# Loading the first batch by another queue: q and k of batch 0 in fp32 by SyncE, A's last products on GpSimd, and a new written order

## The chip, the cores and the metric

The kernel runs on one core of a Trainium2 chip. A core has TensorE (PE, matrix products, with a sequencer row PEld for weight loads), VectorE (DVE), ScalarE (ACT), GpSimd (POOL) and SyncE (SP), which work side by side and wait for each other by semaphores; 16 DMA engines move data between the chip's memory and the core's SBUF. PE writes its results to PSUM, eight banks of 2 KB per partition. The metric is the device time of one execution in microseconds; lower is better.

## The reference

Eight batches of eight heads; 576 tokens of 64 elements per head. A Nystrom attention with 32 landmarks comes first. All inputs are fp32.

```python
q_lm = q.reshape(B, H, 32, 18, 64).mean(axis=3)      # landmarks: mean of 18 tokens
k_lm = k.reshape(B, H, 32, 18, 64).mean(axis=3)
A = softmax(q @ k_lm.T / 8);  Bm = softmax(q_lm @ k_lm.T / 8);  C = softmax(q_lm @ k.T / 8)
Z = Bm.T / (norm1(Bm) * norminf(Bm) + 1e-6)
for _ in range(6):
    Z = 2 * Z - Z @ Bm @ Z
attn = A @ Z @ C @ v
x = attn.transpose(0, 2, 1, 3).reshape(4608, 512)
h = x @ w_in                                         # 512 x 2048
out = relu(h) ** 2 @ w_out                           # 2048 x 512
```

## The kernel before

**The work.** Batches go one after the other through the attention. For each, `attention(b)` makes the landmarks (`lm`), transposes q and k on VectorE (`T`), makes B with its softmax (`B`, `Bmx`, `Bsb`, `Bex`, `Bsu`, `Brc`, `Bml`), the six steps of the inverse (`N` on PE, `U` on VectorE), C (`SC`, `Cmx`, `Cex`, `CT`), C times v (`CV`), Z times that (`Zd`, `Zm`, `ZC`), folds it with `w_in` into one matrix per batch (`W`, copied from PSUM by `We` to `WP`), and makes A with its softmax (`SA`, `Amx`, `Asb`, `Aex`, `Asu`, `Arc`, `Aml`), transposed by `Ap` and copied by `Ab` to `AT`. The feed-forward layer is then `F` (`AT` times `WP`, line 1023), `R` (ReLU, lines 1037 and 1039), `Q` (square, into the buffer `G`, lines 1044 and 1046), and `O` (`G` times `w_out`, line 1063), tile by tile of 128 tokens, `Oe` (copy out of PSUM) and `St` (store by SyncE, line 1076). `F` of a batch overlaps with the attention of the next; G is a ring for two batches.

**Loads.** q and k are loaded by `load_qk` (line 397) in quarters of a batch: t is 0 for q and 1 for k, r is 0 for heads 0 to 3 and 1 for heads 4 to 7. Each is an fp32 block of 128 partitions x 1152 (590 kB), which GpSimd's DMA queue casts on its way to bf16 (288 KB written) in `X[b % 3]`. v (line 413), `w_in` (421), `w_out` (428) and rows of later batches (`XS`, 403) go by the same queue. The queue keeps eight transfers in flight; the ninth issue waits for the first to land, and GpSimd with it.

**Batch 0.** Its two halves of heads are taken apart: heads 4 to 7 first (`lm0.1`, line 480, `SC0.1`), then heads 0 to 3 (`lm0.0`, line 473, and `B0`, which needs both). Batches 0 and 1 make A with the tokens on partitions: a product against a block-diagonal copy of the landmarks (`bk`, line 914; batch 1's is on GpSimd) and a softmax along the free axis. A's last step, `Aml` (line 938), multiplies the exponentials in SBUF (fp32) by the reciprocals of their sums and writes bf16; batch 0 does it in four pieces (two of 256 and two of 320 elements per partition), batch 1 in two (512 and 640).

**The order.** Each step is an `op` with the engines that it may use, a cost on each, what it reads and writes, and for PSUM how many banks. A text `ORDER` lists all of them with the engine (`/A`, `/D`, `/P`) and the bank (`@4`) where there is a choice; a planner (`Plan.schedule`) walks through it, gives each step a start time by its costs, and the instructions are emitted in order of those times. Every engine then works through its own list in order and waits where data is late. The plan's times set the order and nothing else. `fillers` puts products of a matrix of ones (line 1137) into the gaps that the plan shows on PE before the first `O`, so that PE's clock, which the throttle lowers when PE has been idle, stays up.

Of the kernel before, what the change touches and what calls it, by code (L numbers as in the profile page):

```python
# [7 lines left out]
P = 128  # L8
# [45 lines left out]
class Plan:  # L54
# [100 lines left out]

    def fillers(self, until, width, emit):

        busy = sorted((o.start, o.start + o.engs["PE"] + 0.04) for o in self.ops if o.eng == "PE")
        found, at = [], 1.5
        for a, b in busy:  # L160
            if a > until:
                break
            n = int((a - 0.05 - at) / (width if at > 6 else 2 * width))
            if n > 0:
                for j in range(8):
                    if all(h[1] >= a or h[2] <= at - 0.02 for h in self.history if h[0] == j):
                        found.append((at, j, n))
                        break
            at = max(at, b)
        for at, j, n in found:  # L170
            o = Op()
            o.name, o.eng, o.start, o.mode = f"fill{at:.0f}", "PE", at, "full"
# [9 lines left out]
T0 = {"PE": 1.1, "ACT": 1.1, "DVE": 1.1, "POOL": 1.31, "SP": 1.1}  # L182
SW0, LAND, LOADED = 1.5, 1.75, 140.0
# [53 lines left out]
def kernel(  # L237
# [155 lines left out]
    def load_qk(b, t, r):  # L393
# [4 lines left out]
           W=[("X", b % 3, t, r)], nbytes=589824, queue="sw")  # L398
# [8 lines left out]
    def load_v(b):  # L407
        vv = V[b % 3]
        for r in range(2):
            for i, (p0, c0, n) in enumerate(runs(lambda c: pos_c(c, r))):  # L410
# [4 lines left out]
                   W=[("V", b % 3, r, i)], nbytes=147456 * n, queue="sw")  # L415


    def load_win(r, ch):
# [4 lines left out]
           W=[("win", r, ch)], nbytes=524288, queue="sw")  # L423
# [8 lines left out]
    def attention(b):  # L432
        x, tt, lm, lt = X[b % 3], TT[b % 2], LM[b % 2], LT[b % 2]
        kx = lambda t, r: ("X", b % 3, t, r)
# [5 lines left out]
        def transposes(t):  # L440
            for r in range(2):
# [3 lines left out]
                   R=[kx(t, r)], W=[kt(t, r)])  # L445
# [19 lines left out]
        def landmarks(rs):  # L465
# [4 lines left out]
            def lmx(e):  # L470
# [14 lines left out]
               R=["ident", *[kx(t, r) for t in range(2) for r in rs]], W=[pl_], alloc=[pl_],  # L485
# [406 lines left out]
        for u in range(2) if b in TOKENS else ():  # L892
# [28 lines left out]
            for j, (x0, x1) in enumerate(zip(cuts, cuts[1:])):  # L921
# [15 lines left out]
                op(f"Aml{b}.{u}{z}", {"DVE": v_(w)}, lambda e, sa3=sa3, b3=b3, anv=anv, at=at:  # L937
                   nc.vector.tensor_tensor(anv.rearrange("p (x m) -> p x m", m=M)[:, at], sa3[:, at],  # L938
                                           b3(2)[:, at], ALU.mult),
                   R=[*kx_("sa"), *kx_("arc")], W=kx_("An"))  # L940
# [176 lines left out]

    for b in range(4):
        loads("win", b)
        loads("wout", b)  # L1120
    for b in range(B):
        if b in ROWS:
            loads("xs", b)
        loads("kq", b)
# [177 lines left out]
```

## Time and profile before

| | us |
|---|---|
| median of the runs (lowest, highest) | 267.36 (266.87, 269.35) |
| profiled execution | 268.07 |
| its span, first to last instruction | 266.3 |
| busy PE / PEld | 254.8 / 140.4 |
| busy DVE / ACT / POOL | 210.7 / 185.9 / 75.1 |
| mean granted clock of PE | 0.993 |

The profile is of one execution; the span begins with its first instruction. Busy PE includes the fillers (14.1 us in 40 products) and counts a product until its modelled end, so that PE can be held up while it counts as busy. The chain that ended last is followed back from the last instruction, at each step to what released it. In rows of the timeline, "[2.32 <-DMA X<-in_q_dram]" says that the engine had been idle for 2.32 us until a load of q landed; an `x18` behind a row joins 18 instructions.

### The profile page before, as it was taken

The numbers are of one execution on the slowest core, as the hardware profiler recorded it, in microseconds if no ns is written. First come the engines' busy times: TensorE is split into PE (matmuls) and PEld (weight loads), VectorE is DVE, ScalarE is ACT, GpSimd is POOL, SyncE is SP. The second block draws the span as 40 slices with busy tenths as digits, with TensorE's granted clock in tenths as the row PEclk, the third lists the DMA queues.
The fourth block names the chain that finished last, engine by engine and source line by source line (L and its number), as shares of the span: only waits on it lengthen the run. The fifth ranks groups of instructions, "written<-read, shape, count | busy, mean of one in ns | idle before, by whom it ended". The sixth has DMA issues, their size and how long they took to land.

```text
span 266.3 us, 7555 instructions
## 1 busy us (share of the span) xinstructions
PE 254.8 (96%) x3090; PEld 140.4 (53%) x3090; DVE 210.7 (79%) x539; ACT 185.9 (70%) x339; POOL 75.1 (28%) x121
## 2 busy tenths in 40 slices
PE   7699899999999999999999999999999999999993
PEld 2265566466454566455444556456454555456552
DVE  3399999856899889897998889888899895787311
ACT  1055599978687799899597759899586847667120
POOL 8445389346400362026423220210032102000000
PEclk9799999999999999999999999999999999999999
DMA  5999999997998699919996993213250330017016
GB/s 89 195 196 208 203 201 190 205 182 116 157 234 160 120 165 210 182 41 186 225 224 104 193 178 98 47 15 79 51 114 2 83 81 0 2 34 164 2 47 151
DMA packets 25123, 34.18 MB, mean 128 GB/s; under 512 B 2432, under 2 KB 14464, under 8 KB 25088
## 3 DMA queue, kind: packets, MB, share of 16 engines
q0 software_dynamic: 19168, 24.25, 55.7%
q1 hardware_dynamic: 5840, 9.38, 13.8%
q8 instruction: 24, 0.39, 0.6%
q10 hardware_dynamic: 80, 0.07, 0.1%
q14 instruction: 11, 0.09, 0.1%
HBM read 48.50 MB, written 9.44 MB: 218 GB/s over the span
## 4 chain that ended last, share of the span: by engine, by line
PE 73%; DVE 13%; ACT 6%; issue 3%; DMA 3%; POOL 0%; DVEq 0%; POOLq 0%; ACTq 0%
PE ps L1063 40%; PE ps L1023 20%; ACT RS L1037 3%; DMA X<-in_k_dram 3%; PE ps L859 2%; PE ps L702 2%; DVE TT L442 2%; PE ps L788 2%; ACT G L1044 2%; PE ps L1137 1%; DVE sm L740 1%; DVE WP L388 1%; DVE ST L680 1%; PE ps L666 1%; DVE An L938 1%
## 5 line engine op out<-in xcount | busy, mean ns | idle before, releaser
L1063 PE MATMUL ps<-w_out,G 128*128 128x512 bf16 (+1 forms) x592 | 138.5, 374 | 0.1
L1063 PEld LDWEIGHTS <-G 128*128 128x128 bf16 x592 | 54.1, 98 | 53.3 <-issue 5.4
L1023 PE MATMUL ps<-AT,WP 128*128 128x288 bf16 (+2 forms) x512 | 75.0, 286 | 0.9 <-DVE AT L996 0.3
L1037 ACT ACTIVATE RS<-ps 128x576 bf16<-128x576 f32 (+2 forms) x97 | 60.9, 652 | 19.3 <-PE ps L1023 12.0
L1023 PEld LDWEIGHTS <-WP 128*128 128x128 bf16 x512 | 47.9, 98 | 23.8 <-issue 4.3
L1044 ACT ACTIVATE G<-RS 128x576 bf16<-128x576 bf16 (+2 forms) x78 | 52.3, 687 | 0.7
L603 POOL TENSOR_TENSOR BD<-ST,blkb 128x256 bf16<-128x256 bf16 x21 | 14.9, 710 | 85.6 <-DVE ST L680 44.1
L384 ACT COPY OS<-ps 128x512 f32<-128x512 f32 (+2 forms) x29 | 16.2, 567 | 16.7 <-PE ps L1063 16.5
L442 DVE STREAM_TRANSPOSE TT<-X 128x576 uint32<-128x576 uint32 x32 | 23.8, 758 | 5.1 <-DMA X<-in_k_dram 2.8
L1039 DVE TENSOR_SCALAR RS<-ps 128x576 bf16<-128x576 f32 (+2 forms) x31 | 23.1, 754 | 5.4 <-PE ps L1023 5.1
L384 ACT CAST WP<-ps 128x1024 bf16<-128x1024 f32 (+1 forms) x25 | 22.8, 949 | 3.3 <-PE ps L859 3.2
L743 ACT ACTIVATE C<-ps,sm 128x576 bf16<-128x576 f32 x16 | 14.2, 905 | 12.8 <-DVE sm L740 10.8
L1046 DVE TENSOR_TENSOR G<-RS 128x576 bf16<-128x576 bf16 (+2 forms) x42 | 18.8, 452 | 3.6 <-ACT RS L1037 3.4
L680 DVE SCALAR_TENSOR_TENSOR ST<-ST,ps 128x128 bf16<-128x128 bf16 (+1 forms) x48 | 12.7, 264 | 8.2 <-PE ps L666 8.0
L1137 PE MATMUL ps<-onesb 128*128 128x512 bf16 (+1 forms) x40 | 14.1, 470 | 1.8 <-DVE onesb L320 1.5
L413 POOL DMA_DIRECT2D V<-in_v_dram x24 | 13.0, 543 | 7.5 <-DMA X<-in_q_dram 3.5
L388 DVE COPY OS<-ps 128x512 f32<-128x512 f32 (+1 forms) x9 | 5.8, 640 | 10.8 <-PE ps L1063 9.4
L740 DVE TENSOR_REDUCE sm<-ps 128x1 f32<-128x576 f32 x16 | 11.7, 747 | 1.6 <-PE ps L702 1.6
L976 DVE STREAM_TRANSPOSE SA<-ps 128x320 f32<-128x320 f32 (+1 forms) x24 | 10.1, 459 | 3.5 <-PE ps L697 2.4
L603 POOL TENSOR_TENSOR BD<-Bt,blkb 128x256 bf16<-128x256 bf16 x4 | 3.0, 744 | 30.9 <-DVE sm L597 15.0
L1046 POOL TENSOR_TENSOR G<-RS 128x512 bf16<-128x512 bf16 (+1 forms) x8 | 8.8, 1101 | 9.3 <-DVE RS L1039 5.9
L388 DVE CAST WP<-ps 128x1024 bf16<-128x1024 f32 x9 | 10.8, 1205 | 0.8 <-PE ps L859 0.8
(139 smaller groups left out, 303.9 us busy)
## 6 DMA issues: line engine op xcount, KB each, us to landing
out_dram<-OS SPq DMA_DIRECT2D x70, 128.0 KB, 2.4
X<-in_q_dram POOLq DMA_DIRECT2D x16, 288.0 KB, 9.2
X<-in_k_dram POOLq DMA_DIRECT2D x16, 288.0 KB, 9.3
XS<-in_q_dram POOLq DMA_DIRECT2D x5, 576.0 KB, 11.0
XS<-in_k_dram POOLq DMA_DIRECT2D x5, 576.0 KB, 10.2
V<-in_v_dram POOLq DMA_DIRECT2D x8, 288.0 KB, 10.0
w_in<-in_moe_w_in_dram POOLq DMA_DIRECT2D x8, 256.0 KB, 10.6
w_out<-in_moe_w_out_dram POOLq DMA_DIRECT2D x4, 512.0 KB, 10.2
```

The costliest lines, as they stand in the source:

```text
L384: nc.scalar.copy(o, i)
L388: eng(e).tensor_copy(o, i)
L442: op(f"T{b}.{t}{r}", {"DVE": v_(576)}, lambda e, r=r: nc.vector.transpose(tt[:, t, r].rearrange("p s m e -> p (s m e)").bitcast(U32), x[:, ...
L603: bdiag = lambda e, o, i: eng(e).tensor_tensor(o.rearrange("p r (c m) -> p r c m", c=4), i.unsqueeze(2).to_broadcast([P, 2, 4, M]), blkb[: ...
L680: nc.vector.scalar_tensor_tensor(out=o, in0=i0, scalar=2.0, in1=bank(pN)[:, 0:2 * w].rearrange("p (r w) -> p r w", r=2), op0=ALU.mult, op1 ...
L1023: nc.tensor.matmul(ps[:, ph.at + i, 0:w], lhsT=wp[:, r, 128 * ff:128 * ff + 128], rhs=at[:, r, t0:t0 + w], start=(r == 0), stop=(r == 1))
L1037: nc.scalar.activation(rs, pair(ph, w), AF.Relu)
L1039: nc.vector.tensor_scalar(out=rs, in0=pair(ph, w), scalar1=0.0, scalar2=None, op0=ALU.max)
L1044: nc.scalar.activation(g, rs, AF.Square)
L1046: eng(e).tensor_tensor(g, rs, rs, ALU.mult)
L1063: nc.tensor.matmul(bank(po)[:, 0:c1 - c0], lhsT=G[:, f, lo:lo + P], rhs=w_out[:, f, c0:c1], start=(f == 0), stop=(f == NF - 1))
L1137: nc.tensor.matmul(ps[:, j, 0:w], lhsT=onesb[:, 0:P], rhs=onesb[:, 0:w], start=True, stop=True)
```

## The change

Three things. First, the four quarters of q and k of batch 0 are no longer loaded by GpSimd's queue: SyncE loads them in fp32 into planes of `G` that are not in use yet (`load_first`), in the order q0.1, k0.1, k0.0, q0.0, and eight casts of 128 x 576, four on ScalarE and four on VectorE, bring them to `X[0]`. GpSimd's first loads (q and k of batch 1, v of batches 0 and 1, `w_in`) now name the landing of q0.1 as something that they read, so GpSimd waits for it before its first issue; their order is new as well. Second, `Aml` of batches 0 and 1 may go to GpSimd, and all six pieces do. Third, the filler routine chooses by a share of use in any 3.41 us how many products each gap gets (36 products instead of 40), and the whole `ORDER` is another one, with other choices of engine and bank throughout; the planner's start values for SyncE and for GpSimd's queue are other ones too.

```diff
@@ loads
+    def first(t, r):
+        return G[:, 4 * t + 2 * r:4 * t + 2 * r + 2].rearrange("p f n -> p (f n)").bitcast(F32)
+
+    def load_first(t, r):
+        src = (q, k)[t][0, 4 * r:4 * r + 4].rearrange("c (m s) d -> (c m) (s d)", s=SEG)
+        op(f"ld{'qk'[t]}0.{r}", {"SP": 1.5}, lambda e: nc.sync.dma_start(first(t, r), src), W=[("XF", t, r)])
+        for j in range(2):
+            at = slice(576 * j, 576 * j + 576)
+            op(f"cs{t}{r}.{j}", {"DVE": v_(576, True), "ACT": a_(576)}, lambda e, at=at: copy(
+                e, X[0][:, t, r].rearrange("p s d -> p (s d)")[:, at], first(t, r)[:, at]),
+               R=[("XF", t, r)], W=[("X", 0, t, r, j)])
...
-           W=[("X", b % 3, t, r)], nbytes=589824, queue="sw")
+           R=[("XF", 0, 1)] if b < 2 else [], W=[("X", b % 3, t, r, j) for j in range(2)], nbytes=589824, queue="sw")
...
-                    load_qk(b, t, r)
+                    load_qk(b, t, r) if b else load_first(t, r)
@@ A's last product
-                op(f"Aml{b}.{u}{z}", {"DVE": v_(w)}, lambda e, sa3=sa3, b3=b3, anv=anv, at=at:
-                   nc.vector.tensor_tensor(anv.rearrange("p (x m) -> p x m", m=M)[:, at], sa3[:, at],
+                op(f"Aml{b}.{u}{z}", {"DVE": v_(w), "POOL": g_(w)}, lambda e, sa3=sa3, b3=b3, anv=anv, at=at:
+                   eng(e).tensor_tensor(anv.rearrange("p (x m) -> p x m", m=M)[:, at], sa3[:, at],
                                            b3(2)[:, at], ALU.mult),
-                   R=[*kx_("sa"), *kx_("arc")], W=kx_("An"))
+                   R=[*kx_("sa"), *kx_("arc")], W=kx_("An"), port=("POOL", "DVE"))
@@ planner
-T0 = {"PE": 1.1, "ACT": 1.1, "DVE": 1.1, "POOL": 1.31, "SP": 1.1}
-SW0, LAND, LOADED = 1.5, 1.75, 140.0
+T0 = {"PE": 1.1, "ACT": 1.1, "DVE": 1.1, "POOL": 1.31, "SP": 2.9}
+SW0, LAND, LOADED = 6.6, 1.75, 140.0
@@ fillers
+        times = [6.5 + 0.25 * i for i in range(int(4 * (until - 10)))]
+        for _ in range(80):
+            t = min(times, key=share)
+            near = [g for g in gaps if t <= g[0] < t + 3.41 and g[3] - g[0] - g[1] * g[4] > -0.05]
+            if share(t) >= 0.42 or not near:
+                break
+            g = max(near, key=lambda g: g[3] - g[0] - g[1] * g[4])
+            g[1] += 1
@@ the order, its first lines
-c0 ldq0.1 c1 c2 ldk0.1 c3 lm0.1@2 lmc0.10 c12 T0.01 c17 Bce0@5 ldq0.0 ldk0.0 ldq1.0 ldk1.0 c5
-ldq1.1 ldk1.1 c9 c13 c15 T0.11 c6 lmc0.11/D lme0.1 lmt0.1 SC0.1@0 T0.00 Cmx0.1 T0.10 win31 win00
+c0 ldq0.1 c1 c2 c12 c11 cs01.0/A c5 c18 c3 c9 ldq1.0 c6 cs01.1 T0.01 c17 Bce0@0 ldv0.11 ldk0.1
+cs11.1 c13 c15 cs11.0/A lm0.1@2 T0.11 lmc0.10/D lmc0.11/D lme0.1 lmt0.1 SC0.1@2 ldq1.1 ldk1.0
+ldk1.1 ldk0.0 cs10.1/A cs10.0 ldq0.0 cs00.1/A cs00.0 lm0.0@1 T0.10 Cmx0.1 T0.00 T1.00 lme0.0
+lmt0.0 B0@4 ldv0.00 ldv0.10 win10 win00 win11 win31 win01 T1.01 Bmx0 bk0 Bsb0 Bex0 SC0.0@6 Cmx0.0
...
+ldv1.10 bk1/P win30 ldv1.11 ldq2.1 Bsb1 Asu0.0a N0.3@0 U0.3 N0.4@4 CR0@6 Arc0.0a Bex1 Bsu1 Asb0.0b
+Aex0.0b Brc1 CRe0/A Aex0.1b U0.4 Bmb1 Bml1 Btr1 Asu0.0b N0.5@7 U0.5 Zd0@7 Blo1 Bcs1@0 Aml0.0a/P
```

More of the change, by code (lines that the diff above doesn't have):

```diff
@@ L154, in schedule @@
         return max(o.end for o in self.order)
+    USE = {"N": 0.06, "M": 0.06, "B": 0.06, "Bce": 0.28, "Bcs": 0.3, "BBT": 0.08, "SC": 0.2, "CR": 0.06, "lm": 0.48,
+           "SA": 0.78, "CV": 0.63, "Zd": 0.6, "ZC": 0.2, "Ap": 0.54, "W": 0.9}
     def fillers(self, until, width, emit):
[L158 to L161, printed above, removed]
-                break
[L163 to L169, printed above, removed]
@@ L171, in fillers @@
+        for at, n, j, _, unit in gaps:
+            if not n:
+                continue
             o = Op()
-            o.name, o.eng, o.start, o.mode = f"fill{at:.0f}", "PE", at, "full"
+            o.name, o.eng, o.start, o.mode = f"fill{at:.2f}", "PE", at, "full"
             o.engs, o.end = {"PE": n * width}, at + n * width
@@ L1116, in loads @@
             load_wout(b)
+    loads("kq", 0)
     for b in range(4):
@@ L1123 @@
             loads("xs", b)
-        loads("kq", b)
+        if b:
+            loads("kq", b)
         loads("v", b)
```

213 lines of the change are left out of this document (112 added, 101 removed).

## The prediction

> **What bounds the kernel now.** First the page: how long, and what the chain of waits that ended last is made of.
>
> ```profile
> span 266.3 us, 7555 instructions
> ...
> PE 73%; DVE 13%; ACT 6%; issue 3%; DMA 3%; POOL 0%; DVEq 0%; POOLq 0%; ACTq 0%
> ```
>
> Three quarters of the chain is TensorE (PE). It does not say which part of the run is open to a change of the loads, so next comes busy time by stretches (columns: stretch, length, busy of PE, PEld, DVE, ACT, POOL, granted clock, DMA share, GB/s).
>
> ```profile
> 5.00:10.00 5.00, 2.81 (x43) 1.17 (x41) 1.97 (x7) 0.00 (x0) 2.70 (x7) 1.00 1.02 171
> 10.00:15.00 5.00, 4.75 (x42) 2.32 (x43) 3.39 (x8) 1.30 (x5) 2.11 (x6) 0.66 1.10 207
> 16.42:31.86 15.44, 13.86 (x280) 8.50 (x272) 15.34 (x61) 8.14 (x26) 7.98 (x13) 1.00 1.18 205
> 35.00:40.00 5.00, 4.97 (x64) 3.09 (x57) 4.92 (x14) 5.00 (x10) 3.76 (x5) 1.00 1.17 203
> ```
>
> Three stages: until 10 us everything waits for data; from 16.4 to 31.9 VectorE (DVE) is full while PE passes its time with filler products; from 35 ScalarE (ACT) and VectorE are both full and real feed-forward products run. The DMA engines are full from 10 us on in all of them. The chain, in order of time, and four places of the timeline give the marks that I move:
>
> ```profile
> 2.36 6.80 DMA X<-in_k_dram
> 9.30 0.70 PE ps L480 x36
> ...
> 13.45 1.27 PE L473 MATMUL ps<-X,ident 128*128 128x128 bf16 x18
> 16.42 0.22 DVE L533 TENSOR_REDUCE sm<-ps 128x2 f32<-128x64 f32 x1
> 27.73 0.37 DVE L814 TENSOR_TENSOR ZM<-ps,CRS 128x256 bf16<-128x256 f32 x1
> 31.86 0.61 PE L1023 MATMUL ps<-AT,WP 128*128 128x256 bf16 x4
> ```
>
> The first chain piece is k of heads 4 to 7 on its way (the second load). At 9.30 the first landmark product (lm0.1) can start, at 13.45 the second (lm0.0, which needs all four loads), at 16.42 VectorE takes the maxima of B (Bmx0) and begins a chain without a pause that reaches the first feed-forward product (F0) at 31.86.
>
> **The change, part by part.**
>
> *1. Four loads by SyncE.* When GpSimd may issue again shows when old transfers landed (it keeps eight in flight, so its twelfth issue waits for the fourth load, and so on):
>
> ```profile
> 1.31 0.72 POOL L397 DMA_DIRECT2D X<-in_q_dram  x1 [0.79 <-POOLq L1286]
> ...
> 12.27 0.54 POOL L413 DMA_DIRECT2D V<-in_v_dram  x1 [0.40 <-DMA X<-in_k_dram]
> ...
> 15.06 0.62 POOL L421 DMA_DIRECT2D w_in<-in_moe_w_in_dram  x1 [0.86 <-DMA X<-in_k_dram]
> 16.48 0.62 POOL L421 DMA_DIRECT2D w_in<-in_moe_w_in_dram  x1 [0.80 <-DMA X<-in_q_dram]
> ```
>
> The first issue is at 1.31. Load four has landed at 12.27, six and seven at 15.06 and 16.48, 1.42 us apart. No fp32 load by SyncE is in this trace. Its price has bounds from these rows (the waits of SyncE's queue, the DMA issues, the queues):
>
> ```profile
> SPq L1286 <- PEq L1286: 0.7, 1, 0.7
> out_dram<-OS SPq DMA_DIRECT2D x70, 128.0 KB, 2.4
> q1 hardware_dynamic: 5840, 9.38, 13.8%
> ```
>
> SyncE is free at 0.7; a store of 131 kB lands 2.4 us after its issue; a load is 590 kB, 459 more. Rate: hardware-queue packets took 13.8% of 266.3 = 36.7 us for 9.38 MB, 255 kB/us; the upper bound is what the software queue reads, twice the 203 GB/s that it writes in bf16, 406 kB/us. I take 330, between the two. q0.1 then lands at 0.7 + 2.4 + 1.4 = 4.5 (4.2 to 4.9), each further one 1.8 us later (1.45 to 2.3): 6.3, 8.1, 9.9 if alone. They are not alone: GpSimd now waits for q0.1 before its first load, with batch 1's q and k, all of v and w_in, and its own later products behind that wait. In the run before its first bytes moved about 1.4 us after the issue of 1.31 (the row of 2 to 3 us below), so from about 6 us two queues share the engines. The 1.25 MB that SyncE's still has to bring at half of 406 take 6.2 us: the last lands at 12.3, where the fourth landed before. Bounds: 8.6 (406, unshared) and 17.5 (255 alone, then half of that).
>
> Each load is cast in two halves of 128x576, one on ACT, one on DVE, side by side:
>
> ```profile
> L390 DVE TENSOR_SCALAR C<-C,sm 128x576 bf16<-128x576 bf16 x7 | 2.8, 393 | 0.1
> L384 ACT CAST AT<-ps 128x512 bf16<-128x512 f32 x2 | 1.2, 603 | 0.8 <-PE ps L949 0.8
> ```
>
> 0.39 us, or 0.68 with the second row scaled to 576, for a half; I take 0.65. All eight lie where DVE and ACT wait for data (1.97 and 0 busy of 5 above), except the last pair, which is on the path. lm0.1 starts at 6.3 + 0.65 = 7.0 instead of 9.30, lm0.0 at 12.3 + 0.65 = 13.0 instead of 13.45. From lm0.0's end to Bmx0 the old order needed 1.7 us (14.72 to 16.42), for VectorE was still busy with heads 4 to 7; these are now past. lm0.0 (1.0), its copy and transpose (0.5) and one transpose of batch 1 that now stands before Bmx0 (T1.01, 0.77) give Bmx0 at 15.3 to 15.4: **1.0 us gained**. T1.01 needs q1.1, now 6 1/4 loads into the stream: 15.06 + 0.36 = 15.4 by the old pace. The stream runs ahead of the old one by as much as it moves more in the first 6 us:
>
> ```profile
> 2.00:3.00 1.00, 1.00 (x4) 0.38 (x3) 0.50 (x2) 0.09 (x1) 0.91 (x4) 1.00 0.38 32
> 3.00:4.00 1.00, 1.00 (x3) 0.30 (x2) 0.00 (x0) 0.00 (x0) 1.00 (x3) 1.00 0.96 168
> 4.00:5.00 1.00, 1.00 (x4) 0.39 (x3) 0.00 (x0) 0.00 (x0) 1.00 (x3) 1.00 0.93 145
> 5.00:6.00 1.00, 1.00 (x4) 0.37 (x3) 0.72 (x1) 0.00 (x0) 0.93 (x4) 1.00 0.79 136
> ```
>
> That was 481 kB written by 6 us, 0.96 MB read; at 330 kB/us from about 2 us on, 1.32 MB are moved by then, 0.36 MB or 0.9 us at 406 more, say 1.0 with the earlier issue. q1.1 at 14.4 is just in time for a DVE that wants it at 14.5. Without that lead DVE stands up to 1 us there.
>
> *2. A's last products on GpSimd.* From Bmx0 to F0 VectorE is busy 15.34 of 15.44 us (the row above), so what leaves it counts:
>
> ```profile
> 25.36 1.40 DVE L561 TENSOR_TENSOR Bb<-Bl,sm 128x64 bf16<-128x64 f32 x1
> 25.50 1.16 POOL L914 TENSOR_TENSOR BK<-LT,blkw 128x512 bf16<-128x512 bf16 x1
> 27.32 0.38 DVE L938 TENSOR_TENSOR An<-SA,smA 128x256 bf16<-128x256 f32 x1
> 28.02 0.41 DVE L938 TENSOR_TENSOR An<-SA,smA 128x256 bf16<-128x256 f32 x1
> 28.48 0.77 DVE L442 STREAM_TRANSPOSE TT<-X 128x576 uint32<-128x576 uint32 x1
> 29.41 0.87 DVE L938 TENSOR_TENSOR An<-SA,smA 128x320 bf16<-128x320 f32 x2
> ...
> 18.12 0.22 DVE L561 TENSOR_TENSOR Bb<-Bl,sm 128x64 bf16<-128x64 f32 x1
> ...
> 16.12 0.38 DVE L914 TENSOR_TENSOR BK<-LT,blkw 128x512 bf16<-128x512 bf16 x1
> 15.76 0.43 DVE L749 STREAM_TRANSPOSE CT<-C 128x288 uint32<-128x288 uint32 x1
> ```
>
> Gone: batch 0's four products 0.38 + 0.41 + 0.87 = 1.66, T1.01 (moved ahead, paid above) 0.77, and the stall: Bb took 0.22 at 18.12 but 1.40 beside GpSimd's BK, 1.18 more. BK is now behind 15 software loads instead of 22, at the time of A's maxima and subtractions, which read PSUM; I count the stall as gone and keep 1.2 us as its price if it falls on such a product again. Added behind Bmx0: BK 0.38, one CT transpose 0.43. Net 2.80. Rows overlap at their hand-overs (by about 0.1 each), so I count **2.2 us**. On GpSimd the nearest row is
>
> ```profile
> L603 POOL TENSOR_TENSOR BD<-ST,blkb 128x256 bf16<-128x256 bf16 x21 | 14.9, 710 | 85.6 <-DVE ST L680 44.1 <-DVE ST L627 41.5
> ```
>
> 0.7 each for 256, 0.9 for 320. They stand in GpSimd's order behind the issue of batch 2's first load, the 18th, which waits for its tenth to land. Seven loads (4.13 MB) had landed at 16.48; the tenth ends at 7.47 MB (four by SyncE, ten behind them), 8.2 us later at 406, less the lead: 23.7 us, when A's sums are about ready. If it is late by x, the first feed-forward product is late by x.
>
> The Trainium skill's page "SBUF — State Buffer" (Who interferes with whom) says that a VectorE instruction with two SBUF inputs and a GpSimd instruction that reads SBUF exclude each other for the whole instruction. The 1.40 agrees. By it each of the six moved products (two are batch 1's) can block VectorE's next such product; at 1.18 each that would be 7 us against the gain here, and this trace shows one such stall in the stretch.
>
> *3. How much arrives.* F0 would begin 1.0 + 2.2 = 3.2 us earlier. But the second feed-forward matrix is not moved up: the same bytes stand before it.
>
> ```profile
> 34.35 1.58 POOL L428 DMA_DIRECT2D w_out<-in_moe_w_out_dram  x2
> 45.94 1.03 PE L1063 MATMUL ps<-w_out,G 128*128 128x512 bf16 x4
> DMA to landing us min/median/max: 9.5/10.2/11.4
> ```
>
> The first row is the issue of two quarters, the last (of w_out's own view) the time from issue to landing. The first quarter lands at 43.9 to 44.6 and is used at 45.94: 1.4 to 2.1 us of cover, plus the stream's lead of 1.0, is 2.4 to 3.1. PE takes its products in order, so beyond that it waits. **2.7 us** of the 3.2 arrive.
>
> *4. The order after 50 us, and fillers.* Counted in the written order, VectorE takes 11 squares and 5 ReLUs over (8 squares and the ReLUs from ACT):
>
> ```profile
> L1039 DVE TENSOR_SCALAR RS<-ps 128x576 bf16<-128x576 f32 (+2 forms) x31 | 23.1, 754 | 5.4 <-PE ps L1023 5.1
> L1046 DVE TENSOR_TENSOR G<-RS 128x576 bf16<-128x576 bf16 (+2 forms) x42 | 18.8, 452 | 3.6 <-ACT RS L1037 3.4
> ```
>
> 11 at 0.45 and 5 at 0.75 are 8.7 us; its other exchanges (the casts and three output copies against three WP and the six A products) about cancel. PE's products are the same. DVE and ACT carry 13% and 6% of the chain, so I count 0, with 2 us either way. The fillers are 36 instead of 40 and stand at other places; they matter through the clock (0.66 in the row of 10 to 15 above), at a time when VectorE sets the pace: 0, at most 1 us.
>
> Sum: 2.7 us off the profiled execution (268.07 with what lies around its span) is 265.4; off the median of 267.36 it is **264.7**.
>
> **Rivals.**
>
> - *SyncE's loads have the engines to themselves longer, and the new order is as good behind them.* lm0.0 at 9.9 + 0.65, gain 2.9 there, 5 at F0; w_out allows 3.1 plus up to 0.5 of lead, and the rest up to 2: 263.8 to 261.8. For it: the DMA share was below 1 until 6 us. Against: two queues.
> - *Sharing eats the front.* The last load is late, since GpSimd's queue takes half: 14.9 is the point from which lm0.0 (15.6) cancels the 2.2 of part 2. At 17.5 it is 4.7 late, 2.5 net. The four loads at 255 also put the stream behind by 3.4, more than w_out's cover; with one stall of 1.2 on the port this gives 269.9 to 272. For it: k's load took 6.80 us in company, in the chain's first row. Against: at the middle rate it stays hidden.
> - *VectorE becomes the bound.* The 8.7 us that it takes over fall partly on stretches where it was full; half on the chain is 4.3 less the 2.7: 269, or 268 to 270.6.
> - *Nothing is won at the loads.* Only part 2 remains, limited by the cover of 1.4 to 2.1 without a lead: 265.6. The Trainium skill's page "DMA: Bandwidth & Descriptors" (Issuing engines are not separate DMA queues) states as much: all queues run on the same 16 engines and only issue time is saved. The shares near 1 above bear it out from 6 us on, not before.
>
> **How the numbers follow.** A change of 1%, 2.7 us, is about what can be told from none. Forecast 0.36 (own range 263.2 to 266.2, more than half below 264.7), loads alone 0.20, sharing 0.21, VectorE 0.13, nothing won 0.10. Faster: 0.22 + 0.20 = 0.42. Slower: 0.21 + 0.06 = 0.27. The rest, 0.31, is within 1%. The range reaches from 261.0 to 271.5.
>
> **What would show it.** Right: lm0.1 at about 7, lm0.0 near 13, Bmx0 near 15.4, the first product of F0 at 28 to 29, the first of w_out at 43 to 43.5, and the same distance to the end. Wrong: lm0.0 after 15, GpSimd's first An after 26, PE waiting on w_out by more than 1 us, or ground lost between 50 and 250 with a chain that has more of VectorE.

## The result, and the profile after

| | before | after |
|---|---|---|
| median of 20 runs each, us | 268.06 | 266.38 |
| lowest, highest | 265.19, 270.69 | 264.97, 267.02 |
| profiled execution, its span | 268.07, 266.3 | 266.46, 264.7 |

The ratio of after to before is 0.9933, 95% interval [0.9911, 0.9955]: 0.7% less time, about 1.8 us, where 2.7 were forecast. The interval excludes no change, and the gain is still within the 1% that the prediction named as hardly to be told from none. The lowest times are alike; what differs is the upper end, 270.69 against 267.02.

The changed kernel's page, its length and the chain that ended last; then its busy time by stretches (columns as before: stretch, length, busy of PE, PEld, DVE, ACT, POOL, granted clock, DMA share, GB/s):

```profile
span 264.7 us, 7514 instructions
...
PE 69%; DVE 16%; ACT 10%; issue 4%; ACTq 0%
```

```profile
5.00:10.00 5.00, 2.89 (x43) 1.71 (x44) 3.48 (x11) 2.19 (x5) 2.38 (x5) 0.76 1.04 314
14.60:30.31 15.71, 14.24 (x277) 8.69 (x271) 14.45 (x59) 8.00 (x22) 8.88 (x14) 0.82 1.18 198
21.00:23.00 2.00, 1.12 (x50) 0.59 (x36) 2.00 (x9) 0.93 (x3) 2.00 (x4) 1.00 1.24 204
24.00:25.00 1.00, 1.00 (x13) 0.38 (x11) 1.00 (x7) 0.82 (x4) 0.00 (x0) 0.82 1.03 167
25.00:30.00 5.00, 4.87 (x69) 2.52 (x69) 4.04 (x14) 2.38 (x5) 3.69 (x6) 0.50 1.20 208
```

Two things stand out against the rows of before. The engines that move data write 314 GB/s between 5 and 10 us instead of 171, since the four loads of SyncE are written in fp32. And PE's granted clock, 1.00 throughout this stretch in the profile before, is 0.50 from 25 to 30 us, after a stretch (21 to 23) in which PE has work for 1.12 of 2 us. The marks that the prediction moved, from the timeline of the changed kernel:

```profile
7.39 1.05 PE L511 MATMUL ps<-X,ident 64*64 64x128 bf16 x36
11.79 1.17 PE L504 MATMUL ps<-X,ident 128*128 128x128 bf16 x18
30.31 1.03 PE L1054 MATMUL ps<-AT,WP 128*128 128x256 bf16 x4
45.14 1.03 PE L1094 MATMUL ps<-w_out,G 128*128 128x512 bf16 x3
14.60 0.18 DVE L564 TENSOR_REDUCE sm<-ps 128x2 f32<-128x64 f32 x1
```

| mark | before | forecast | after | gain so far |
|---|---|---|---|---|
| lm0.1 | 9.30 | 7.0 | 7.39 | 1.9 |
| lm0.0 | 13.45 | 13.0 | 11.79 | 1.7 |
| Bmx0 | 16.42 | 15.3 to 15.4 | 14.60 | 1.8 |
| first F0 | 31.86 | 28 to 29 | 30.31 | 1.55 |
| first O | 45.94 | 43 to 43.5 | 45.14 | 0.8 |
| end of span | 266.3 | | 264.7 | 1.6 |

So the front gained more than forecast, the stretch from Bmx0 to F0 gained nothing (15.71 us against 15.44) where 2.2 were forecast, 0.75 went between F0 and the first product with `w_out`, and the rest of the run is 0.8 shorter.

Of the 20 executions, ten show a mean granted clock of 0.997 or more (median 265.4 us) and ten one of 0.978 to 0.993 (median 266.6). The profiled one, 0.978, has the lowest of all: its clock is at 0.50 from 7.6 to 11.0 us and again from 24.6 to 31.5. The other nine of the slower ten, at 0.990 or more, had about half of that or less; where, a mean doesn't say.

One thing said of the change and in the prediction doesn't hold: GpSimd doesn't wait for q0.1. The read of q0.1 that the loads on its queue now name only tells the planner to place them later; no semaphore comes of it. The row of GpSimd's first load, and VectorE's cast at the landing of q0.1, say so:

```profile
2.86 0.73 POOL L416 DMA_DIRECT2D X<-in_q_dram  x1
4.51 0.46 DVE L407 CAST X<-G 128x576 bf16<-128x576 f32 x1 [1.67 <-DMA G<-in_q_dram]
```

The issue is at 2.86, 1.65 us ahead of the landing.

### The profile page after: what moved, and what is told of

Read it like the earlier page. It is cut to its first block, busy times and chain, and to the rows that moved or that the text cites. A ratio compares the mean times of both kernels' runs of the same rounds, so it can differ in the third digit from the quotient of the medians.

```text
span 264.7 us, 7514 instructions
## 1 busy us (share of the span) xinstructions
PE 250.3 (95%) x3047; PEld 141.3 (53%) x3086; DVE 213.8 (81%) x559; ACT 181.5 (69%) x328; POOL 71.5 (27%) x116
## 4 chain that ended last, share of the span: by engine, by line
PE 69%; DVE 16%; ACT 10%; issue 4%; ACTq 0%
PE ps L1094 36%; PE ps L1054 20%; PE ps L890 3%; ACT RS L1068 3%; ACT G L1075 2%; PE ps L1170 2%; PE ps L733 1%; DVE RS L1070 1%; DVE An L1024 1%; PE ps L819 1%; PE ps L489 1%; DVE TT L473 1%; ACT WP L403 1%; DVE sm L771 1%; DVE SA L1007 1%
## 5 line engine op out<-in xcount | busy, mean ns | idle before, releaser
L1094 PE MATMUL ps<-w_out,G 128*128 128x512 bf16 (+1 forms) x556 | 132.7, 373 | 3.1 <-issue 1.9
L1068 ACT ACTIVATE RS<-ps 128x576 bf16<-128x576 f32 (+2 forms) x92 | 57.9, 650 | 17.8 <-PE ps L1054 15.6
L1075 ACT ACTIVATE G<-RS 128x576 bf16<-128x576 bf16 (+2 forms) x70 | 46.8, 683 | 5.3 <-DVE RS L1070 4.3
L1070 DVE TENSOR_SCALAR RS<-ps 128x576 bf16<-128x576 f32 (+2 forms) x36 | 26.7, 748 | 8.2 <-PE ps L1054 6.1
L403 ACT CAST WP<-ps 128x1024 bf16<-128x1024 f32 (+1 forms) x28 | 26.2, 972 | 4.9 <-PE ps L890 4.9
L1077 DVE TENSOR_TENSOR G<-RS 128x576 bf16<-128x576 bf16 (+2 forms) x53 | 23.2, 451 | 7.0 <-ACT RS L1068 6.6
L1170 PE MATMUL ps<-onesb 128*128 128x512 bf16 (+1 forms) x33 | 11.5, 462 | 2.1 <-DVE onesb L339 1.5
L890 PE MATMUL ps<-w_in,ZC 64*32 64x512 bf16 x256 | 11.9, 397 | 0.4 <-DVE ST L711 0.2
L1018 DVE TENSOR_REDUCE smA<-SA 128x20 f32<-128x640 f32 (+1 forms) x12 | 8.8, 738 | 2.3 <-ACT SA L1016 2.1
L1024 DVE TENSOR_TENSOR An<-SA,smA 128x640 bf16<-128x640 f32 (+1 forms) x12 | 10.1, 842 | 0.2
```

What stands on the lines that cost most here:

```text
L403: nc.scalar.copy(o, i)
L890: nc.tensor.matmul(ps[quad(pos_a(c, r)), pW.at + r, :], lhsT=zcs[r][half, pos_c(c, r), :], rhs=w_in[half, c, 512 * ch:512 * ch + 512], sta ...
L1068: nc.scalar.activation(rs, pair(ph, w), AF.Relu)
L1070: nc.vector.tensor_scalar(out=rs, in0=pair(ph, w), scalar1=0.0, scalar2=None, op0=ALU.max)
L1075: nc.scalar.activation(g, rs, AF.Square)
L1077: eng(e).tensor_tensor(g, rs, rs, ALU.mult)
```

## The experiments

Theories at the start: *the loads* bring what Bmx0 gained; *the clock* eats what the A products on GpSimd should have brought ahead of F0. Rivals: the products on GpSimd stall VectorE through the port that they share, and the new order as a whole gains or loses. The runs were made on three chips. On the first (more fillers, all six back on VectorE, loads back to GpSimd, SyncE's loads alone) the median of the kernel before was 266.98, on the second (fewer fillers, products alone, real wait, the front's small order) 267.65, on the third (the other four) 267.57. Kernels on one chip are compared directly, others by their ratio to the kernel before.

### The clock

**More fillers.** Four products of ones more in the changed kernel, where PE stood still:

```diff
+            free = free or BANK.get(o.name, [])
+        for g in gaps:
+            g[1] += EXTRA.get(g[5], 0)
+EXTRA, BANK = {'N0.3': 5, 'N0.4': 2}, {'N0.3': [6]}
```

> The changed kernel with four more filler products (5 and 2 units of 256 columns ahead of the inverse's fourth and fifth step of batch 0, at 21.3 to 23.3 us, where PE stood for 0.88 us). Theory 'the clock ate it': PE's granted clock stays at 1.00 from 24.8 to 30.9 us instead of 0.50, the first F0 comes 1.0 to 1.5 us before 30.31, and the kernel ends at 265.0 to 265.6, about 1 us under the changed kernel. Theory 'VectorE sets the pace there whatever the clock': the clock is back, F0 moves by less than 0.3 and the time is the changed kernel's. Theory 'use of PE is not what lowers the clock': it still falls to half between 24 and 31 us.

Measured: 265.45 (265.24 to 266.36), ratio 0.9934 [0.9905, 0.9963]; 11 of 12 executions at a clock of 0.994 or more. By stretches:

```profile
14.60:30.31 15.71, 14.30 (x293) 8.79 (x281) 14.99 (x60) 7.69 (x22) 8.86 (x14) 1.00 1.18 195
21.00:23.00 2.00, 1.76 (x74) 0.94 (x57) 1.98 (x8) 0.93 (x3) 2.00 (x4) 1.00 1.23 204
25.00:30.00 5.00, 4.10 (x74) 2.30 (x73) 4.52 (x17) 2.42 (x7) 3.68 (x6) 1.00 1.20 209
```

With 1.76 of 2 us in use at 21 to 23, the clock stays at 1.00. VectorE, which had been busy 4.04 of 5 us behind a slow PE, is busy 4.52. Bmx0 to F0 takes 15.12 us (14.80 to 29.92) instead of 15.71, F0 to the first O 14.55 instead of 14.83. So the half clock costs 0.9 us in this pair of profiles, and 265.45 is what the changed kernel takes in its own executions at full clock (265.4). At F0 itself 0.4 came (29.92 instead of 30.31) of the 1.0 to 1.5 that the first theory expected; the time is within the 265.0 to 265.6 that it named. But the ratio to before is the changed kernel's (0.9934 and 0.9933), so that a lower median isn't shown; what is shown is that the slower half of the executions goes.

**Fewer fillers in the kernel before.** The counter-test: 12 products at 21 to 25 us left out.

```diff
         for at, j, n in found:
+            if 19 < at < 24.5:
+                continue
```

> The kernel before without its filler products from 21.3 to 25.2 us (12 products fewer), nothing else changed. Theory 'low use of PE there costs the clock a few us later': the granted clock falls to about a half from some 24 to 31 us, as in the changed kernel, F0 comes 1 to 1.5 us later than 31.86 and the time is 0.7 to 1.5 us above the kernel before. Theory 'VectorE sets the pace whatever the clock': clock or not, within 0.3 us.

Measured: 268.84 (265.99 to 269.74), ratio 1.0039 [1.0008, 1.0070], 1.0 us more than before. The clock falls as expected:

```profile
22.00:24.00 2.00, 0.97 (x39) 0.43 (x36) 2.00 (x11) 0.99 (x4) 1.06 (x3) 1.00 1.22 203
25.50:31.50 6.00, 5.02 (x133) 3.64 (x133) 5.96 (x25) 1.80 (x6) 3.54 (x6) 0.50 1.17 209
```

But VectorE is busy 5.96 of 6 us beside the half clock, Bmx0 to F0 takes 15.39 us (17.57 to 32.96) against 15.44 at full clock, and the profile's later end was there by Bmx0 already: 17.57 instead of 16.42, with the fourth load landing 0.4 us later and a half clock from 8.4 to 15.2 us, ahead of the fillers that were left out. The low use of PE lowers the clock: shown. What a half clock costs where VectorE is full is left open: the runs say about 1 us, and this profile doesn't show where.

### A's last products

**All six back on VectorE** in the changed kernel:

```diff
-... Aml0.0a/P ... Aml0.0b/P ... Aml0.1a/P ... Aml0.1b/P ... Aml1.1/P ... Aml1.0/P
+... Aml0.0a ... Aml0.0b ... Aml0.1a ... Aml0.1b ... Aml1.1 ... Aml1.0
```

> The changed kernel with A's six last products back on VectorE. By step 2 of the prediction they are worth 1.66 us of VectorE's time ahead of F0: 1.0 to 1.7 us slower than the changed kernel, 267.5 to 268. Theory 'the clock ate it': VectorE waits for PE at 25 to 30 us anyway (0.73 of every us busy at 25 to 26), so 0 to 0.7 slower. Rival 'the products on GpSimd stall VectorE by the shared port': 0.3 to 1 us faster than the changed kernel, with the seam (line 655 at 26.78, 0.58 us) back at 0.2.

(At 25 to 26 us VectorE of the changed kernel was idle for 0.73 of the 1 us, not busy, as the expectation has it.) Measured: 266.64 (266.42 to 267.62), above every execution of the kernel with more fillers, whose clock was likewise full: 1.2 us slower than that at the medians, ratio 0.9988 [0.9959, 1.0016] to before. The filler routine set some more products here of its own accord and the clock stayed at 1.00, so the pair with more fillers is the fair one. F0 comes at 29.74, *earlier* than the 29.92 with the products on GpSimd, and the first O at 45.39 instead of 44.47. The six products are worth 1.2 us in this order, and nothing of it shows at F0.

**Only batch 1's two on GpSimd**, with the additional fillers, tests whether the 1.2 us lie in batch 1's two large products:

```diff
-... Aml0.0a/P ... Aml0.0b/P ... Aml0.1a/P ... Aml0.1b/P
+... Aml0.0a ... Aml0.0b ... Aml0.1a ... Aml0.1b
```

> The changed kernel with the additional fillers and with only batch 1's two last products of A on GpSimd; batch 0's four are back on VectorE (the filler routine then chooses some more products). Theory 'only batch 1's two are worth something': F0 at 29.6 to 30.0 as with all six on GpSimd, and 265.2 to 265.8, the time of the kernel with more fillers. Theory of step 2 (batch 0's four are worth 1.66 us ahead of F0): F0 at 31 or later and 266.4 to 267.

Measured: 266.30 (266.18 to 267.12), ratio 0.9961 [0.9939, 0.9982]; F0 at 30.01, the first O at 44.74. At F0 the expectation holds: batch 0's four products, 1.66 us of VectorE, are worth 0.1 us there. The total doesn't hold: it lies above the 265.2 to 265.8 expected and just under the 266.4 of the other theory, at full clock (0.996 or more in 11 of 12). By the ratios, 0.9934 with all six on GpSimd, 0.9961 with batch 1's two and 0.9988 with none, each group is worth about 0.7 us, with intervals that overlap; at the first O of the three profiles (44.47, 44.74, 45.39) batch 0's four are worth 0.27 and batch 1's two 0.65. So how the 1.2 us divide isn't shown; that batch 0's four bring next to nothing at F0 is. Why they are worth so little there shows in the timelines of VectorE, GpSimd and PE in the kernel with more fillers (first), and of VectorE with batch 0's products on itself (second):

```profile
26.70 0.86 DVE L658 TENSOR_TENSOR ST<-Bf,sm 128x64 bf16<-128x64 f32 x1
...
25.57 0.62 POOL L972 TENSOR_TENSOR An<-SA,smA 128x256 bf16<-128x256 f32 x1 [1.29 <-DVE smA L970]
26.12 0.60 POOL L419 DMA_DIRECT2D X<-in_q_dram  x1
26.74 0.74 POOL L972 TENSOR_TENSOR An<-SA,smA 128x320 bf16<-128x320 f32 x1
...
27.56 0.54 PE L983 MATMUL ps<-ident,An 128*128 128x128 bf16 x3 [0.84 <-issue]
```

```profile
25.25 0.41 DVE L972 TENSOR_TENSOR An<-SA,smA 128x256 bf16<-128x256 f32 x1
...
25.82 0.43 DVE L972 TENSOR_TENSOR An<-SA,smA 128x256 bf16<-128x256 f32 x1
...
27.14 0.22 DVE L658 TENSOR_TENSOR ST<-Bf,sm 128x64 bf16<-128x64 f32 x1
...
28.21 0.88 DVE L972 TENSOR_TENSOR An<-SA,smA 128x320 bf16<-128x320 f32 x2
```

The step of the inverse that runs beside GpSimd's product takes 0.86 instead of 0.22: 0.64 of the 1.66 us go back. And GpSimd's third product stands behind a load's issue (0.60) and takes 0.74, where VectorE does two in 0.88; it ends at 27.48, and PE stands for 0.84 us until 27.56 in the middle of the transposes of A (the profile names no releaser there).

**The products alone, in the kernel before**:

```diff
-                op(f"Aml{b}.{u}{z}", {"DVE": v_(w)}, ...
+                op(f"Aml{b}.{u}{z}", {"DVE": v_(w), "POOL": g_(w)}, ...
```
(all six with `/P` at the places where the old order has them)

> The kernel before with only the second part: A's six last products on GpSimd at the same places of the order, loads and fillers as before. By step 2 of the prediction 1.66 us leave VectorE ahead of F0, of which the cover of 1.4 to 2.1 us at w_out lets as much through: 266.4 to 267.2 against 268.1. Rival 'the port': VectorE's neighbours with two SBUF inputs grow by 0.4 to 1.2 us each beside the products and the time is 268 to 269. Rival 'GpSimd is late': its products wait behind the issues of loads that wait for landings, F0 at 32 or later, 268.5 or more.

Measured: 274.30 (271.48 to 276.46), ratio 1.0218 [1.0173, 1.0263], 5.8 us slower by the ratio. GpSimd and PE:

```profile
28.91 0.53 POOL L413 DMA_DIRECT2D V<-in_v_dram  x1 [1.16 <-DMA X<-in_q_dram]
29.46 2.55 POOL L938 TENSOR_TENSOR An<-SA,smA 128x256 bf16<-128x256 f32 x4
27.00 4.17 PE L1137 MATMUL ps<-onesb 128*128 128x512 bf16 x19 [0.52 <-issue]
33.64 0.75 PE L1023 MATMUL ps<-AT,WP 128*128 128x256 bf16 x4
```

All four products come in one piece at 29.46, behind load issues that wait for landings; PE passes the time with fillers and VectorE has no work from 27.5 to 33. "GpSimd is late" is the rival that held, far above the 268.5 that it named. F0 is 1.8 us later than before, and the first O 6.3 us (52.28): batch 1's first product stands on GpSimd at 40.91 only, and from 44 to 52 us GpSimd is busy for 7.95 of 8 us, with the clock at 0.57. On this engine a product is worth what stands in front of it, and the new order is a condition of the second part.

### The loads

**Back to GpSimd's queue**, in bf16, in the changed kernel; no casts:

```diff
-c0 ldq0.1 c1 c2 c12 c11 cs01.0/A c5 c18 c3 c9 ldq1.0 c6 cs01.1 T0.01 ... ldk0.1
+c0 ldq0.1 c1 c2 ldk0.1 ldq0.0 ldk0.0 c12 c11 c5 c18 c3 c9 ldq1.0 c6 T0.01 ...
```

> The changed kernel with batch 0's q and k again loaded by GpSimd's queue in bf16, without the eight casts and without the fp32 loads by SyncE; the rest of the order stands. Theory 'the loads brought the gain': lm0.1 back at 9 to 9.5, lm0.0 at 13.3 to 14, Bmx0 at 15.8 to 16.5, and 1.5 to 2 us slower than the changed kernel, 268 to 268.5. Rival 'nothing won at the loads': the same time as the changed kernel, since all transfers share the same engines and the casts cost as much as the earlier landing.

Measured: 266.31 (265.41 to 268.98), ratio 0.9985 [0.9951, 1.0018]; the kernel with more fillers, on the same chip, had 265.45 (265.24 to 266.36). So 0.9 us slower at the median, by the ratios 1.4 from the changed kernel; but the profile is not what was expected:

```profile
7.42 0.70 PE L511 MATMUL ps<-X,ident 64*64 64x128 bf16 x36 [0.53 <-DMA X<-in_k_dram]
10.71 1.18 PE L504 MATMUL ps<-X,ident 128*128 128x128 bf16 x18
14.55 0.18 DVE L564 TENSOR_REDUCE sm<-ps 128x2 f32<-128x64 f32 x1
```

lm0.0 stands at 10.71, a microsecond *ahead* of SyncE's loads, and this execution took 265.41, the lowest of its twelve. The other executions range up to 268.98, and they go with the clock: three at a mean of 1.00 took 265.4 to 265.8, seven at 0.992 to 0.994 took 266.0 to 267.5, two at 0.984 or less 267.7 and 269.0. At full clock the kernel with more fillers takes the same (265.4 to 265.9 at 0.996 or more), so there the two ways of loading cost the same. The suspicion: where GpSimd's queue loads first, the landing itself varies. The kernel before had its loads in the same way in the runs with fewer fillers and with products on GpSimd, so two of its landings were known; two more profiles of it, unchanged (no edit):

> The kernel before once more, unchanged, for another profile of its loads. Theory 'where GpSimd's queue loads first, the landing itself spreads from execution to execution': lm0.1 anywhere from 7.4 to 9.7 and lm0.0 from 10.7 to 14.6, with the span following. Rival 'the kernel before always lands at 9.3 and 13.45': within 0.2 us of these.

> The kernel before a third time, as the run ahead of it: lm0.1 from 7.4 to 9.7 and lm0.0 from 10.7 to 14.6 by the theory of the spread, 9.3 and 13.45 within 0.2 us by its rival.

Measured: 267.69 (267.06 to 269.91) and 267.96 (265.98 to 270.51), ratios 1.0020 [0.9987, 1.0054] and 1.0002 [0.9962, 1.0041]. lm0.1 and lm0.0 of the two:

```profile
8.73 0.70 PE L480 MATMUL ps<-X,ident 64*64 64x128 bf16 x36 [2.06 <-DMA X<-in_k_dram]
12.99 1.17 PE L473 MATMUL ps<-X,ident 128*128 128x128 bf16 x18
```

```profile
9.28 0.70 PE L480 MATMUL ps<-X,ident 64*64 64x128 bf16 x36 [2.02 <-DMA X<-in_k_dram]
12.12 1.17 PE L473 MATMUL ps<-X,ident 128*128 128x128 bf16 x18
```

| loads first by GpSimd's queue, old order | before | again | again | fewer fillers | A on GpSimd |
|---|---|---|---|---|---|
| lm0.1 | 9.30 | 8.73 | 9.28 | 9.70 | 7.67 |
| lm0.0 | 13.45 | 12.99 | 12.12 | 14.60 | 10.95 |
| Bmx0 | 16.42 | 16.13 | 15.29 | 17.57 | 14.24 |

| loads by SyncE, new order | after | A on VectorE | more fillers | batch 1's A on GpSimd |
|---|---|---|---|---|
| lm0.0 | 11.79 | 11.80 | 11.88 | 11.95 |
| Bmx0 | 14.60 | 14.73 | 14.80 | 14.81 |

The same first loads put lm0.0 anywhere within 3.65 us in one group and within 0.16 in the other. But the start of lm0.0 isn't the landing. GpSimd's twelfth issue waits for the fourth load; it stands at 12.27, 11.69, 12.23, 12.65 and 11.19 us in the five profiles, a spread of 1.46. The rest is PE's clock. Ahead of lm0.1 PE was idle for 2.19, 2.06, 2.02, 3.52 and 0.46 us; in the first, second and fourth profile the granted clock then fell to 0.50 for 3.4 us or more, and lm0.0 stands behind products that PE takes at that clock. The kernel before and its third profile are a pair: lm0.1 at 9.30 and 9.28, the twelfth issue at 12.27 and 12.23, but lm0.0 at 13.45 and 12.12. One of PE's products ahead of it, in the first and in the third:

```profile
11.98 1.15 PE L702 MATMUL ps<-TT,LT 32*32 32x288 bf16 x16
```

```profile
12.23 0.54 POOL L413 DMA_DIRECT2D V<-in_v_dram  x1 [0.38 <-DMA X<-in_k_dram]
11.28 0.69 PE L702 MATMUL ps<-TT,LT 32*32 32x288 bf16 x16
```

In the second group, too, lm0.0 stands behind PE's own products; there the casts of the last load begin at 10.49 to 10.97.

At Bmx0 the means are 15.9 and 14.7: the loads, and the new order in front of Bmx0 with them, are worth 1.2 us on average. The two aren't told apart by this (SyncE's loads in the old order, below, have Bmx0 at 16.17). The profile that the prediction was made against was a late one, by its clock more than by its landing.

An earlier Bmx0 doesn't reach the end by itself. The third profile has it 1.13 us ahead of the first, but F0 at 31.85, as the first, and its span (266.0 against 266.3) hardly follows: its clock is at 0.50 from 28.0 to 31.4 us, and VectorE waits for a copy that stands behind PE:

```profile
30.98 0.29 DVE L680 SCALAR_TENSOR_TENSOR ST<-ST,ps 128x128 bf16<-128x128 bf16 x1 [0.67 <-ACT WP L384]
```

The clock goes with the width of the runs, 265.2 to 270.7 before and 265.0 to 267.0 after. On the first chip the kernel before took 265.26 (median) in eleven executions at a mean clock of 0.996 or more, 267.52 in nineteen at 0.989 to 0.994 and 268.73 in five at 0.987 or less; on the other two chips it was 266.3 (two each), 267.5, and 268.4 to 268.7. At full clock, then, it was as fast on the first chip as the kernel with more fillers there (265.45). What differs is how often: 15 of 93 executions before, 10 of 20 after. This sorts executions by what came out of them and is no experiment; an early landing and a full clock come together in it.

What in the queue makes the landing itself vary isn't settled; the issues stand at the same places in all five profiles (1.31, 2.36, 2.95, ...).

**SyncE's loads alone, in the kernel before**, the casts ahead of lm0.1 and lm0.0:

```diff
-c0 ldq0.1 c1 c2 ldk0.1 c3 lm0.1@2 lmc0.10 c12 T0.01 c17 Bce0@5 ldq0.0 ldk0.0 ldq1.0 ...
+c0 ldq0.1 c1 c2 ldk0.1 c3 ldq0.0 ldk0.0 c12 cs01.0/A cs01.1 cs11.0/A cs11.1 lm0.1@2 lmc0.10 T0.01 ...
```

> The kernel before with only the first part: batch 0's q and k by SyncE in fp32, eight casts ahead of lm0.1 and lm0.0; the old order and filler routine otherwise, A's products on VectorE. Theory 'the loads bring 1.6 to 1.8 us': lm0.0 at 11.5 to 12.3, F0 at 30.2 to 30.6, 266.2 to 266.6 against 268.1. Rival 'the loads need the new order': lm0.0 earlier, but VectorE has heads 4 to 7 in front of Bmx0 and F0 moves by less than 0.7: 267.4 to 268. Rival 'sharing': v and batch 1 land later by GpSimd's queue and the whole is slower than before.

Measured: 267.79 (266.95 to 269.21), ratio 1.0040 [1.0006, 1.0075], 1.1 us slower, with a narrower range than before's 265.02 to 269.63 on that chip. lm0.1 comes at 6.98, lm0.0 at 12.62:

```profile
1.92 0.73 POOL L397 DMA_DIRECT2D X<-in_q_dram  x1
...
11.90 0.46 DVE L388 CAST X<-G 128x576 bf16<-128x576 f32 x1 [2.07 <-DMA G<-in_k_dram]
...
13.61 1.42 DVE L454 STREAM_TRANSPOSE TT<-X 128x576 uint32<-128x576 uint32 x2
...
16.17 0.21 DVE L545 TENSOR_REDUCE sm<-ps 128x2 f32<-128x64 f32 x1
```

GpSimd issues its first load at 1.92, 0.94 earlier than in the changed kernel, and the last of SyncE's lands at 11.9 instead of 10.5 (with a first issue at 5.08, in the next run, at 9.3). From lm0.0 to Bmx0 it takes 3.55 us, where the kernel before took 2.97 and the changed one 2.8: in the old order the transposes of k and q stand behind the last cast and in front of Bmx0. Both rivals hold a part: sharing, and the need for the new order.

**A real wait.** GpSimd copies two elements of q0.1's plane before its first load:

```diff
+        op("see", {"POOL": 0.2}, lambda e: nc.gpsimd.tensor_copy(seen[:], first(0, 1)[:, 0:2]),
+           R=[("XF", 0, 1)], W=["seen"])
-... c18 c3 c9 ldq1.0 ...
+... c18 c3 c9 see ldq1.0 ...
```

> The changed kernel with a small copy on GpSimd that reads the first load's plane ahead of its own first load, so that GpSimd really waits for q0.1, as the prediction had it. Theory 'queues share': SyncE's four loads then have the engines alone until about 6 us; k0.0 and q0.0 land 0.3 to 0.8 earlier (10.47 to about 9.8), GpSimd's stream runs 1 to 1.5 us later, w_out with it, and the time is within 0.4 us of the changed kernel or up to 1 us slower, where v or batch 1's q and k are late for VectorE. Rival 'the first bytes of GpSimd's queue do not matter': lm0.0 as in the changed kernel, same time.

Measured: 265.59 (264.80 to 266.74), ratio 0.9929 [0.9902, 0.9956]: the changed kernel's.

```profile
5.08 0.73 POOL L417 DMA_DIRECT2D X<-in_q_dram  x1
10.30 1.17 PE L509 MATMUL ps<-X,ident 128*128 128x128 bf16 x18
13.87 0.18 DVE L569 TENSOR_REDUCE sm<-ps 128x2 f32<-128x64 f32 x1
```

GpSimd's first issue moves from 2.86 to 5.08, lm0.0 from 11.79 to 10.30 and Bmx0 by 0.73, but F0 (29.78) by 0.53 and the first O (44.56) by 0.58, at a clock that again fell to 0.50.

### Both, and the front's small order

**Real wait and more fillers** together, the two edits above in one kernel:

> The changed kernel with both: GpSimd's real wait for q0.1 and the four filler products more. Theory 'front and clock are two separate costs': lm0.0 near 10.3 as with the wait alone, granted clock 1.00 through 21 to 31 us, the first product of w_out at 43.6 to 44.0 and 264.4 to 265.0. Rival 'the end of the front is set elsewhere' (w_out's landing or the softmax of A): the first product of w_out not before 44.4, and 265.3 to 265.6 as with either alone.

Measured: 265.27 (264.85 to 265.91), ratio 0.9914 [0.9885, 0.9943], the lowest median and the lowest ratio of all. The clock is 1.00, lm0.0 at 10.29, Bmx0 at 13.62, F0 at 29.60, the first O at 44.19: between the two expectations, closer to the rival's. Bmx0 to F0 takes 15.98 us now, 0.9 longer than without the wait. VectorE's timeline shows what took it:

```profile
23.54 0.56 DVE L600 TENSOR_TENSOR Bb<-Bl,sm 128x64 bf16<-128x64 f32 x1
24.02 0.63 DVE L582 TENSOR_TENSOR Bf<-Bl,sm 128x64 f32<-128x64 f32 x1
26.61 1.03 DVE L663 TENSOR_TENSOR ST<-Bf,sm 128x64 bf16<-128x64 f32 x1
```

The same three took 0.22, 0.22 and 0.86 with more fillers alone: 0.9 us more of the stall beside GpSimd's products, since these now meet two more of VectorE's.

**The front's small order.** The old filler routine in the changed kernel, ScalarE's first cast ahead of its copies of constants, and VectorE's second ahead of a transpose:

```diff
-c0 ldq0.1 c1 c2 c12 c11 cs01.0/A ... cs01.1 T0.01 c17 Bce0@0 ldv0.11 ldk0.1 cs11.1 c13
+c0 ldq0.1 c1 c2 c12 cs01.0/A ... cs01.1 c17 Bce0@0 ldv0.11 ldk0.1 cs11.1 T0.01 c13
```

> The changed kernel with the old filler routine (31 products, fewer still at 20 to 27 us), with ScalarE's cast of q0.1 ahead of its copies of constants and VectorE's cast of k0.1 ahead of the transpose of q0.1. Theory 'the front is set by ScalarE's and VectorE's order': lm0.1 at 6.5 to 7.0 instead of 7.39, lm0.0 little changed (it needs the last load at 10.47): Bmx0 within 0.4 of 14.60. Theory 'the clock': with the old routine the half clock from 24.8 on stays or lasts longer, so the whole is 0 to 1 us slower than the changed kernel.

Measured: 266.40 (264.78 to 267.02), ratio 0.9948 [0.9927, 0.9968]. lm0.1 6.83, lm0.0 11.30, Bmx0 14.63 and F0 30.33, where the changed kernel has 14.60 and 30.31: the earlier lm0.1 is worth nothing by Bmx0. Ten of the twelve executions have a clock of 0.990 or less, and the time is that of the changed kernel's slower half.

## Why the prediction was right or wrong

**The sum.** The sign was right and the size, 1.8 us against the kernel before instead of 2.7, is two thirds of the forecast; 264.7 was 1.7 us low, and the forecast's own range (to 266.2) ends 0.2 below the median. That it came so near is in part luck: 0.8 us more than forecast at Bmx0 made up for some of the 2.2 that didn't come behind it.

**1. The loads: the sign right, the size too small, a mark misread, and a wait that isn't there.** Bmx0 gained 1.8 us in the two profiles where 1.0 was forecast, 1.2 in the mean of more profiles, the new order in front of it included. q0.1 landed at the 4.5 that was worked out, with the 367 GB/s of the row below between the 330 that the step took and its upper bound of 406. The last load landed at 10.5 instead of 12.3 (the cast of q0.0, second row, starts with it): three loads of 590 kB in the 6.0 us behind 4.5 are 295 kB/us, more than the half of 406 that the step left to SyncE's queue.

```profile
2.00:5.00 3.00, 3.00 (x10) 1.03 (x8) 1.12 (x4) 2.92 (x8) 2.86 (x8) 1.00 0.97 367
```

```profile
10.49 0.67 ACT L403 CAST X<-G 128x576 bf16<-128x576 f32 x1 [2.14 <-DMA G<-in_q_dram]
```

"GpSimd now waits for q0.1" was wrong, as shown; with a real wait lm0.0 stands at 10.30, the 10.55 that the first rival had worked out. The sentence on the Trainium skill's page "DMA: Bandwidth & Descriptors" (Issuing engines are not separate DMA queues) would have had no gain here beyond the time of issue. At full clock, as in the run with lm0.0 at 10.71, it is borne out; in the medians, 0.9 us apart, it isn't. What no step had asked is whether 13.45, read from one execution, was a typical mark, and whether it was the landing at all: the fourth load had landed by 12.27, and a half clock stood between.

**2. A's products: the step that failed.** 2.2 us were expected ahead of F0. At full clock, in the kernel with more fillers, the stretch from Bmx0 takes 15.12 us instead of 15.44 (14.90 in another profile of the kernel before), and the four products of batch 0 brought 0.1 of that, with GpSimd in time as forecast (its first product at 23.3 in the changed kernel). The mechanism that failed is "what leaves VectorE counts". Against the profile before, VectorE's own list in the stretch holds what the sum lacked: 0.64 came back as the stall that had been priced at 1.2 and set aside, 0.34 as one beside BK, 0.25 is a step of the inverse more, and VectorE waits for 0.72 us where it waited for 0.10. Together that is 1.85 us, about the 1.9 that are missing. Next in line was PE, waiting for GpSimd's slower product. The page "SBUF — State Buffer" (Who interferes with whom) of the Trainium skill agrees with the stalls (0.22 to 0.86 and to 1.03 beside a product of GpSimd), but the 7 us estimated from it, all six at 1.18, didn't come. The 1.2 us that the six are worth at the end stand in no term of the sum: it had batch 1's two among the exchanges of step 4 that cancel. BK's stall shrank without going: beside BK (20.42, 1.16 us) VectorE's CMX product took 0.52 where it took 0.17 before.

**3. The cover at `w_out`** was never used up: F0 came 1.55 us earlier, not 3.2, and PE didn't wait for `w_out`. Between F0 and the first O 0.75 was lost, 0.28 of it to the half clock; the chain of waits in that stretch runs over VectorE's ReLU, a CMX product beside GpSimd's square (at 36.18, 0.99 us; before it took 0.59) and ScalarE's copies, where it ran on PE before. Which exchange of the new order costs the other half microsecond wasn't tried.

**4. The order behind and the fillers.** "0, with 2 us either way" was right: from the first O to the end the span holds 220.4 us before (220.3 in both repeats) and 219.6 after, a gain of 0.8. "0, at most 1 us" for the fillers was at its edge: the half clock costs the changed kernel 0.9 in the profiles and 1.2 between its own executions.

**The rivals.** "Sharing eats the front" and "VectorE becomes the bound" didn't come; the first is seen, in small, where SyncE's loads stand in the old order. "Nothing won at the loads" fell in the medians, and holds at full clock. "Loads to themselves" needs the real wait, and even then little of its 1.5 us at lm0.0 reaches the end.

## What to carry to other kernels

A duration taken from one profile is one draw: before a transfer's landing becomes a term of a sum, look at the spread of the kernel's runs, and where that is several times what is to be gained, profile it again. Ask, too, whether a product began late because its data was late or because of what stood ahead of it on its engine, and at which clock. A step moved to a slower engine is worth what that engine has in front of it and what runs beside it, not what the faster engine loses: the same six products were worth 1.2 us in one order and cost 5.8 in another. A read in a planner's list is no wait; look in the timeline whether the engine stood still.

## What the runs showed of the hardware

- The fourth of four loads of 590 kB that GpSimd's queue casts to bf16 landed between 11.19 and 12.65 us in five profiles, at equal issue times; with SyncE's fp32 loads of the same data, started at 0.81, the casts of the last one began at 10.49 to 10.97 in four.
- A stretch of 2 us in which PE had work for 1.12 was followed by a half granted clock from 24.6 to 31.5 us; at 1.76 of the same 2 us the clock stayed at 1.00. In two executions of one program PE was idle for 2.19 and 2.02 us at the same place, and the clock fell in the first alone. In ten of twenty executions of the same program the mean clock stayed at 0.997 or above. The Trainium skill's page "TensorE: Matmul & The Clock Gate" (What's actually happening) states that the activity window runs freely, without regard to the kernel's start; with these counts that agrees, and a gap that sits near the limit is then a matter of the execution.
- A VectorE product of two SBUF operands of 128x64, 0.22 us alone, took 0.56, 0.63, 0.86 and 1.03 beside products of GpSimd of 0.61 to 0.74 us, and 1.40 beside one of 1.16.
